# Attention, dense layer and routed experts on one core: moving a logarithm to GpSimd, loading the first head pair on two queues, and gathering the first expert's rows before the last token group is finished

## The chip, the cores and the metric

The kernel runs on one core of one Trainium2 chip. Its time is the device time in microseconds (us) of one execution, and the number quoted is the median over several executions. The engines of the core are TensorE (PE; its weight loads are listed as PEld), VectorE (DVE), ScalarE (ACT), GpSimd (POOL) and SyncE (SP, which here only starts DMA transfers).

## The reference

Three layers follow each other, all in float32. `B, H, S, D` are 4, 8, 576, 64; there are 2304 tokens of 512 numbers, a dense layer of width 2048, and 8 experts of width 1024 that take exactly 288 tokens each.

```python
scores = q @ k.T / sqrt(D);  cum = cumsum(log(clip(f, 1e-4, 1)))
scores = where(causal, -1e9, scores + cum[:, None] - cum[None, :])
attn   = exp(scores - max);  attn /= attn.sum(-1) + 1e-9
x = (attn @ v) as (2304, 512)
h = x @ w_in;  x = max(0.01 * h, h) @ w_out
# routing: all (token, expert) logits x @ w_gate in falling order; a token goes to
# the first expert in that order that still has room, 288 tokens per expert
out[mask_e] = relu(x[mask_e] @ w1[e]) @ w2[e]
```

`w_in`, `w_out` and `w_gate` belong to the dense layer and the routing, `w1` and `w2` to the experts. `w_in` and `w_out` arrive as float64 and are turned into float32 on the chip by integer operations.

## The kernel before

Most products are made of three float32r products of high and low parts (high by high, high by low, low by high), so that each float32 operand is first split: a copy to float32r is the high part, a subtraction the low part.

**Attention.** It works on 16 pairs of heads. For each pair `prepare` loads k and q, transposes them on PE, splits them into `kh, kl, qh, ql`, and loads two rows of the cumulated logarithm into `kr`. `offsets` makes the scores with queries on the partitions, takes the maxima on DVE (`kept`, `nm`) and the sums of the exponentials on ACT (`sm`), and then the logarithm of the sums: `guess` (DVE), `ratio` (ACT, an exponential) and `series` (DVE, six small operations on a tile `ln` of 128x10). `rows` transposes the result and writes it by DMA into `qr`. `attend` makes the scores again with keys on the partitions, now with the offset already in the product, exponentiates them on ACT (`P`), clears what is not causal on GpSimd, multiplies with v, and `finish` splits the result (`xt`) and stores it. Meanwhile the first half of `w_in` is decoded from float64, partly on DVE (`wbits`), partly on GpSimd (`wsq`, `wst`, low part of `wh`).

All of this is written as operations of a `Plan` with an engine, a duration, needs and a rank. `Plan.order` simulates the engines and rings of buffers and so fixes the order of instructions on each engine; on the chip each engine keeps that order. The constants `ZP` to `ZB` are the ranks, `MW`, `ZW`, `DW` the places of the decoding.

At the start, the zeros and ones that pad `qr`, `kr`, `kh`, `kl`, `qh`, `ql` are set by GpSimd (`pads`). The logarithm of f is cumulated, negated, split and written to DRAM (`cumd`), from where `kr` of each pair is loaded.

**Dense layer.** A first half of the width is computed after the attention and stored to DRAM (`gd`), then a second half is computed and kept in SBUF (`g1s`). Both are multiplied with `w_out` later, by the generator `deferred`: 9 groups of 256 tokens, 96 matmuls of 128x512 each, 864 in all. Groups 0 to 6 are taken one by one, groups 7 and 8 together. Every finished group is copied to `xo` by ACT and stored to `x2d` in DRAM.

**Routing.** The generator `routing` finds the assignment with many small DVE operations and small matmuls. It yields estimated nanoseconds. After each yield, as many matmuls of `deferred` are put into PE's stream as fit: `PACE` times the estimate, divided by 228 ns (lines 1035 to 1042). What is left comes after the routing. The result is `ids`, 96x24 token numbers, three columns per expert.

**Experts.** `fetch(e)` loads and splits the weights of an expert, `gather(e)` fetches its 288 rows of `x2d` by three indirect DMAs from GpSimd's queue, `turn` transposes them on PE into the operand `X[e]`, and `first` (tile `h`) and `after` (tile `y`) are the two products. For expert 0 all of that begins after the last store of `x2d`; the rows of each further expert are gathered while the expert before it is computed.

## Time and profile before

| | |
|---|---|
| median of 3 runs | 941.02 us (940.88 to 943.09) |
| the profiled execution, its own time | 943.13 us |
| its span (first to last instruction) | 941.10 us |
| PE, PEld, DVE, ACT, POOL busy | 95%, 81%, 65%, 43%, 47% of the span |
| mean granted TensorE clock | 0.979 of full speed |

The span is made of stages that follow each other: attention to 213 us, the dense layer's first products to 454 us, routing with the deferred products to 696 us, and the experts to the end. Busy shares are means over these stages, which have different limits; they have to be read stage by stage. A matmul's end is modelled, so that a busy PE is not necessarily a PE at its peak.

### The profile page before, as it was taken

What the parts mean: (1) busy time and instruction counts of PE and PEld (TensorE: products, weight loads), DVE (VectorE), ACT (ScalarE), POOL (GpSimd) and SP (SyncE); (2) the same over time, 40 slices, a digit from 0 to 9 for tenths busy, and PEclk for the clock granted to TensorE, in tenths of its full rate; (3) what the DMA queues carried; (4) which work ended last, traced back from release to release, by engine and by line L of the source; (5) the groups of instructions that cost most, each with busy time, mean ns of one, the idle gap of its engine ahead of it and who ended that gap; (6) DMA issues with size and microseconds to landing.
All of it is one profiled execution on the core that took longest, in us unless ns stands there. A gap on an engine that the chain in (4) does not pass through costs nothing.

```text
span 941.1 us, 19011 instructions
## 1 busy us (share of the span) xinstructions
PE 893.4 (95%) x6906; PEld 759.8 (81%) x6906; DVE 609.9 (65%) x1552; ACT 407.2 (43%) x949; POOL 438.4 (47%) x548
## 2 busy tenths in 40 slices
PE   6899899999999999999999999999959999999996
PEld 5688787887877887777777777777649999999996
DVE  6899999845789369523466766667735666566631
ACT  5988778861222223312222222123314555555521
POOL 8265666345999149100645655468752122221101
PEclk9999999999999999999899999999889999999998
DMA  5455565369985473521212221121336556556511
GB/s 130 105 156 157 143 161 141 95 196 294 334 298 173 156 222 117 178 90 45 85 62 69 68 68 49 65 68 49 116 126 192 175 187 193 191 185 204 182 41 33
DMA packets 139677, 131.81 MB, mean 140 GB/s; under 512 B 68448, under 2 KB 106656, under 8 KB 139584
## 3 DMA queue, kind: packets, MB, share of 16 engines
q1 hardware_dynamic: 136512, 121.17, 41.8%
q0 software_dynamic: 3072, 9.44, 3.4%
q8 instruction: 54, 0.88, 0.4%
q14 instruction: 39, 0.32, 0.1%
HBM read 99.85 MB, written 30.56 MB: 139 GB/s over the span
## 4 chain that ended last, share of the span: by engine, by line
PE 69%; DVE 11%; issue 11%; POOL 4%; ACT 3%; DMA 1%; POOLq 0%; SPq 0%; ACTq 0%; DVEq 0%
PE acc L1031 21%; PE h L71 21%; PE h L1087 7%; PE s L71 7%; PE y L1100 6%; PE T L71 3%; DVE kept L71 3%; DVE ln L71 3%; PE q_ct L1031 2%; DVE wbits L71 2%; ACT kept L71 2%; POOL out L1108 1%; DVE r_ge L1249 1%; DVE xt L71 1%; PE T L1077 1%
## 5 line engine op out<-in xcount | busy, mean ns | idle before, releaser
L71 PE MATMUL h<-X,wh 128*128 128x512 f32 (+1 forms) x960 | 211.1, 376 | 0.9 <-DVE g L71 0.9
L71 PEld LDWEIGHTS h<-X,wh 128*128 128x128 f32 x960 | 166.1, 189 | 38.4 <-DVE g L71 3.0
L1031 PE MATMUL acc<-wh,gh 128*128 128x512 f32 x576 | 190.3, 406 | 0.0
L461 POOL TENSOR_TENSOR gl<-g,gh 128x512 fp32r<-128x512 f32 x64 | 104.1, 1631 | 75.5 <-ACT gh L460 72.3
L1031 PEld LDWEIGHTS acc<-wh,gh 128*128 128x128 f32 x576 | 108.8, 193 | 19.5
L1087 PE MATMUL h<-XE,wh 128*128 128x288 f32 x768 | 118.3, 303 | 0.3 <-ACT XE L1078 0.3
L71 DVE TENSOR_TENSOR wh<-wst,wh 128x512 fp32r<-128x512 f32 x132 | 90.5, 707 | 42.8 <-ACT wh L360 31.2
L1031 PE MATMUL acc<-wh,gl 128*128 128x512 f32 x288 | 116.9, 406 | 0.0
L360 ACT CAST wh<-wst 128x512 fp32r<-128x512 f32 x132 | 80.4, 621 | 79.9 <-DMA wst<-in_moe_w 47.2
L1087 PEld LDWEIGHTS h<-XE,wh 128*128 128x128 f32 x768 | 106.5, 191 | 0.6 <-ACT XE L1078 0.6
L460 ACT CAST gh<-g 128x512 fp32r<-128x512 f32 x64 | 39.5, 621 | 141.6 <-PE acc L1031 127.1
L71 ACT ACTIVATE g<-h 128x512 f32<-128x512 f32 (+1 forms) x72 | 39.5, 551 | 139.0 <-PE h L71 136.8
L1100 PE MATMUL y<-eh,wh 128*128 128x288 f32 x512 | 98.4, 296 | 0.0
L71 ACT ACTIVATE kept<-kept,nm 128x192 f32<-128x192 f32 (+4 forms) x160 | 87.8, 551 | 17.1 <-DVE nm L71 16.9
L1108 POOL DMA_INDIRECT out<-yo,ids x24 | 24.7, 1028 | 129.3 <-DVE yo L1107 120.1
L1100 PEld LDWEIGHTS y<-eh,wh 128*128 128x128 f32 x512 | 79.5, 188 | 0.2 <-ACT eh L1091 0.2
L71 DVE TENSOR_TENSOR g<-g,h 128x512 f32<-128x512 f32 (+1 forms) x72 | 44.6, 621 | 51.9 <-ACT g L71 51.9
L71 DVE SCALAR_TENSOR_TENSOR wbits<-w,wbits 128x256 int32<-128x256 int32 x128 | 75.3, 589 | 2.8
L71 POOL TENSOR_TENSOR wst<-wsq,wbits 128x256 f32<-128x256 f32 x64 | 49.8, 779 | 46.4 <-DVE wbits L71 42.3
L1100 PE MATMUL y<-el,wh 128*128 128x288 f32 x256 | 67.9, 296 | 0.0
L1031 PEld LDWEIGHTS acc<-wh,gl 128*128 128x128 f32 x288 | 55.4, 192 | 9.8
L71 POOL TENSOR_SCALAR wsq<-wsq 128x256 f32<-128x256 f32 x64 | 59.9, 935 | 5.6
(210 smaller groups left out, 1605.3 us busy)
## 6 DMA issues: line engine op xcount, KB each, us to landing
wst<-in_moe_w SPq DMA_DIRECT2D x128, 256.0 KB
X<-xd SPq DMA_DIRECT2D x12, 1024.0 KB
g<-gd SPq DMA_DIRECT2D x36, 256.0 KB
w<-in_moe_w_in SPq DMA_DIRECT2D x32, 256.0 KB
w<-in_moe_w_out SPq DMA_DIRECT2D x32, 256.0 KB
gd<-g SPq DMA_DIRECT2D x16, 512.0 KB
xd<-xt SPq DMA_DIRECT2D x16, 320.0 KB
x2d<-xo SPq DMA_DIRECT2D x18, 256.0 KB
```

Source lines behind the costliest of these rows:

```text
L71: r = getattr(self.engine, name)(*a, **k)
L360: A.copy(r[u][0], x)
L460: A.copy(gh, g)
L461: G.tensor_tensor(gl, g, gh, op=OP.subtract)
L1031: tc.keep_in_program_order(PE.matmul(*a, **k))
L1077: PE.transpose(p[:, M * t:M * t + M], xe[t][:, 128 * c:128 * c + 128], ident[:M, :M])
L1087: PE.matmul(h[:, :CAP], w, X[:, c, x, :], start=n == 0, stop=n == 3 * NC - 1)
L1100: PE.matmul(yt[c][:, :CAP], w[:, s], a, start=j == 0 and n == 0, stop=j == NJ - 1 and n == 2)
L1108: sd = G.indirect_dma_start(out=out[:, :], out_offset=bass.IndirectOffsetOnAxis(ap=ids[:, 3 * e + t:3 * e + t + 1], axis=0), in_=y, in_off ...
L1249: V.scalar_tensor_tensor(many[:, :NT * (K + 1)].rearrange("p (i k) -> p i k", k=K + 1)[:, :, :K], key[:, :, None].to_broadcast(s), base if ...
```

## The change

Seven things change.

1. In `offsets`, the first guess of the logarithm goes from DVE to ACT, and the series from DVE to GpSimd, where it is nine small instructions (one for `ready`, eight for `series`) in place of six.
2. `FIN`: the high part of the first 320 queries of each pair (`xt`) is copied by ACT instead of DVE.
3. For pair 0, q is loaded on ACT's DMA queue while k is loaded on SP's; `kr` of pair 0 is copied straight from the negated tile in SBUF, not from `cumd`; its `KR` pads are set by DVE. The memsets and the load of `w_gate`, and `sel`, move behind the attention.
4. The planner's ranks change, and `PACE` goes from 1.1 to 1.05.
5. `deferred` takes all nine groups one by one. In the last, the low parts of g are made by DVE instead of GpSimd, and its sums stay in PSUM.
6. The rows of the last group in `x2d` are set to zero beforehand. Expert 0's rows are gathered right after `ids`, while the last group is still being multiplied; when all but 24 of its matmuls are in PE's stream, PE transposes them as products with the identity into four PSUM tiles `px`. When the last group is done, its two 128x512 tiles are split (`Y`) and multiplied with one-hot matrices (`sel8`, made from the ranks `df`) into the same `px`: 16 matmuls of 128x288. `px` is then split into the operand `X0`. The stores of the last group to `x2d` come after that.
7. `g1s` becomes one tile per piece of `WIDE2`, so that `ax`, `X0` and `Y` can take the place of finished pieces.

```diff
-ZP, ZO, ZA, ZH, ZL, ZW, DW = -38, -27, 5, -6, -14.5, 68.5, 15.5
-ZS = 7, 3.5, 7, 1, 3.5, 11.5, 15.5
+ZP, ZO, ZA, ZH, ZL, ZW, DW = -39, -27, 5, -9.5, -10.5, 63, 14.5
+ZS = 5, 5.5, 7, 0.5, 2.5, 11, 11.5
-FIN = ("vec", "vec"), ("vec", "gp")
+FIN = ("act", "vec"), ("vec", "gp")
-PACE = 1.1
+PACE = 1.05
+QS = "sp", "aq"
...
-    G.memset(wgs, 0.0)
-    with nc.allow_non_contiguous_dma(reason="small"):
-        nc.sync.dma_start(wgs[:, :, :E], w_gate.rearrange("(c p) e -> p c e", p=128))
...
+            on = (vec, "vec") if n == 0 else (gp, "gp")
...
+            at_q = (sp, act) if n == 0 else (sp, sp)
...
-                sp.dma_start(x3[j][:, :, i], src[b, h + i, :512].rearrange("(t p) d -> p t d", p=128))
+                at_q[j].dma_start(x3[j][:, :, i], src[b, h + i, :512].rearrange("(t p) d -> p t d", p=128))
...
+                if n == 0:
+                    outs[0].append(op("sp", 450, lambda l=u: sp.dma_start(kr[l:l + 65:64, :S].bitcast(FT), pre["cn"][l][:2].bitcast(FT)), [negs[u]] + pads[0], z + 1, (), [sets[0]], 30))
+                    continue
...
-            def guess():
-                own["ln"] = x = at.tile([128, 3, 10], FT, name="ln", tag="ln", bufs=2)
-                vec.tensor_scalar(x[:, 0], own["sm"].bitcast(I32), LN[0], LN[1], op0=OP.mult, op1=OP.add)
-
             def ratio():
-                act.activation(own["ln"][:, 1], own["ln"][:, 0], AF.Exp)
+                own["ln"] = x = at.tile([128, 4, 10], FT, name="ln", tag="ln", bufs=2)
+                act.activation(x[:, 0], own["sm"].bitcast(I32), AF.Copy, scale=LN[0], bias=LN[1])
+                act.activation(x[:, 1], x[:, 0], AF.Exp)
+
+            def ready():
+                x = own["ln"]
+                gp.tensor_scalar(x[:, 3], own["sm"], 1e-9, None, op0=OP.add)
 
             def series():
                 x, t = own["ln"][:, 2], own["ln"][:, 1]
-                vec.scalar_tensor_tensor(t, own["sm"], 1e-9, t, op0=OP.add, op1=OP.mult)
-                vec.tensor_scalar(x, t, LN[5], LN[4], op0=OP.mult, op1=OP.add)
-                vec.tensor_tensor(x, x, t, op=OP.mult)
-                vec.scalar_tensor_tensor(x, x, LN[3], t, op0=OP.add, op1=OP.mult)
-                vec.scalar_tensor_tensor(x, x, LN[2], own["ln"][:, 0], op0=OP.add, op1=OP.add)
-                vec.tensor_tensor(x, x, own["nm"][:, :10], op=OP.add)
+                gp.tensor_tensor(t, own["ln"][:, 3], t, op=OP.mult)
+                gp.tensor_scalar(x, t, LN[5], LN[4], op0=OP.mult, op1=OP.add)
+                gp.tensor_tensor(x, x, t, op=OP.mult)
+                gp.tensor_scalar(x, x, LN[3], None, op0=OP.add)
+                gp.tensor_tensor(x, x, t, op=OP.mult)
+                gp.tensor_scalar(x, x, LN[2], None, op0=OP.add)
+                gp.tensor_tensor(x, x, own["ln"][:, 0], op=OP.add)
+                gp.tensor_tensor(x, x, own["nm"][:, :10], op=OP.add)
...
-        for gs in [[g] for g in range(NG - 2)] + [[NG - 2, NG - 1]]:
+        for g in range(NG):
...
+                    gh, gl = split_g(x, V if g == NG - 1 else G)
...
-        for _ in rest:
-            pass
+                dealt.append(1)
+        def deal(n):
+            while len(dealt) < n and next(rest, None):
+                dealt.append(1)
+        deal(96 * NG - 92)
+        ax = g1p.tile([128, 4, 512], FT, name="xe", tag="g1a", bufs=1)
...
+        for t in range(2):
+            V.tensor_scalar(sel8[t], ax[:, 3, :CAP], where[0][:, NT - 2 + t:NT - 1 + t], None, op0=OP.is_equal)
+        gather(0, [ax[:M, t] for t in range(3)])
...
+        deal(96 * NG - 24)
+        for t in range(3):
+            for c in range(NC):
+                mm(px[c][:, M * t:M * t + M], ax[:M, t, 128 * c:128 * c + 128], ident[:M, :M], start=t == 0, stop=False)
+        deal(96 * NG)
+        Y = g1p.tile([128, 4, 2, 512], FR, name="Y", tag="g1b", bufs=1)
+        for t in range(2):
+            A.copy(Y[:, t, 0], last[t])
+            V.tensor_tensor(Y[:, t, 1], last[t], Y[:, t, 0], op=OP.subtract)
+        for l in range(2):
+            for t in range(2):
+                for c in range(NC):
+                    mm(px[c][:, :CAP], Y[:, t, l, 128 * c:128 * c + 128], sel8[t], start=False, stop=l == t == 1)
+        for c in range(NC):
+            part_operand(X0, c, px[c])
+        for t in range(2):
+            leave_first(NG - 1, t, last[t])
...
-        xe = {0: gather(0)}
-        X = {0: operand()}
-        for c in range(NC):
-            turn(X[0], xe[0], c)
+        xe = {}
+        X = {0: X0}
```

## Rows read from the trace of the kernel before

**Rows 1.** Windows by stage: us, busy us (instructions) per engine, granted clock, DMA.

```profile
25.00:205.00 180.00, 165.05 (x1971) 144.39 (x1967) 156.66 (x613) 150.74 (x445) 96.35 (x158) 0.98 0.54 145
454.00:692.60 238.60, 233.98 (x1617) 181.18 (x1614) 160.52 (x353) 57.93 (x97) 147.08 (x124) 0.97 0.22 72
```

**Rows 2.** The chain that ended last, 25 to 205 us, shares by line.

```profile
by line: PE s L71 27.0%; DVE kept L71 16.2%; DVE ln L71 13.6%; issue 9.6%; ACT kept L71 7.4%; DVE wbits L71 6.8%; DVE xt L71 4.4%; DVE ql L71 2.6%; ACT kh L71 1.9%; ACT qh L71 1.8%; DVE nm L71 1.6%; DVE X L71 1.4%; DMA x<-in_k 1.0%; DVE kl 
```

**Rows 3.** Windows inside the attention, columns as in rows 1.

```profile
175.00:200.00 25.00, 24.51 (x314) 21.65 (x312) 19.06 (x79) 21.30 (x60) 9.09 (x20) 1.00 0.62 180
60.00:170.00 110.00, 100.92 (x1213) 88.54 (x1215) 101.29 (x384) 91.13 (x271) 70.02 (x108) 0.98 0.57 152
```

**Rows 4.** Tile ln: ns min/median/max, first and last start.

```profile
L71 DVE SCALAR_TENSOR_TENSOR ln<-ln x32: 169/314/1295, 25.2 to 195.9; 128x10 f32<-128x10 f32 x32
L71 DVE TENSOR_SCALAR ln<-sm x16: 159/166/599, 23.9 to 194.4; 128x10 f32<-128x10 int32 x16
```

**Rows 5.** Tile ln in one window: us, then busy PE, PEld, DVE, ACT, clock, DMA.

```profile
0.00:205.00 205.00, 4.50 (x16) 1.36 (x16) 35.54 (x112) 3.34 (x16) 0.98 0.55 144
```

**Rows 6.** Tiles r_nr and xt, columns as in rows 4.

```profile
L1298 POOL TENSOR_SCALAR r_nr<-r_rp x7: 255/261/403, 489.1 to 673.9; 128x8 f32<-128x8 f32 x7
...
L71 DVE CAST xt<-s x14: 474/479/491, 46.2 to 199.5; 128x320 fp32r<-128x320 f32 x14
```

**Rows 7.** Timeline at 112 us, GpSimd and DVE: start, us, instruction.

```profile
111.99 1.29 POOL L71 TENSOR_TENSOR wh<-wst,wh 128x512 fp32r<-128x512 f32 x1
112.01 1.29 DVE L71 SCALAR_TENSOR_TENSOR ln<-ln 128x10 f32<-128x10 f32 x1
```

**Rows 8.** Timeline of the first 13 us.

```profile
6.42 0.75 DVE L71 SCALAR_TENSOR_TENSOR kept<-cum,kept 32x576 fp32r<-32x576 f32 x1
...
7.15 0.89 SPq L71 DMA_DIRECT2D cumd<-kept  x2
...
8.38 1.55 DVE L71 SCALAR_TENSOR_TENSOR X<-s,X 128x512 fp32r<-128x512 f32 x4 [1.21 <-ACT X L71]
...
11.17 0.59 SPq L71 DMA_DIRECT2D X<-cumd  x2
...
13.01 0.93 PE L71 MATMUL s<-X,qo 64*128 64x192 f32 x2 [0.18 <-POOL qr L71]
```

**Rows 9.** Waits between 460 and 692 us: total us, times, longest.

```profile
DVE r_jk L1258 <- PE q_ct L1031: 49.2, 34, 5.2
...
PEld L1031 <- DVE r_ge L1249: 7.9, 17, 2.5
```

**Rows 10.** Timeline from the routing's last matmuls to expert 0.

```profile
692.20 0.41 PE L1031 MATMUL q_misc<-r_ge 128*96 128x48 bf16 x6
...
692.86 0.18 DVE L71 SCALAR_TENSOR_TENSOR ids<-q_misc,r_kf 96x24 int32<-96x24 f32 x1
...
695.53 0.39 PE L1031 MATMUL acc<-wh,gl 128*128 128x512 f32 x1
699.58 1.17 POOL L1069 DMA_INDIRECT xe<-x2d,ids  x1 [8.23 <-DMA x2d<-xo]
...
703.06 0.56 PE L1077 MATMUL T<-ident,xe 96*128 96x96 f32 x2 [7.14 <-DMA xe<-x2d,ids]
...
705.47 0.58 PE L1077 MATMUL T<-ident,xe 96*128 96x96 f32 x2 [0.70 <-DMA xe<-x2d,ids]
...
709.72 0.40 ACT L1078 CAST XE<-T 128x288 fp32r<-128x288 f32 x1 [1.57 <-PE T L1077]
...
712.46 1.32 PE L1100 MATMUL y<-eh,wh 128*128 128x288 f32 x8
```

**Rows 11.** One window there, columns as in rows 1.

```profile
700.00:708.00 8.00, 3.34 (x13) 2.50 (x14) 0.82 (x2) 0.96 (x3) 5.37 (x6) 0.50 0.46 132
```

**Rows 12.** Pieces of the chain on PE: start us, us, what.

```profile
488.66 11.01 PE acc L1031 x48
...
719.43 1.59 PE y L1100 x12
```

More of the change, by code (lines that the diff above doesn't have):

```diff
@@ L96 @@
            ("vec", "act"): 205, ("vec", "gp"): 155, ("act", "gp"): 180}
-    MOVE = 650, 2200
+    MOVE = 650, 2600
     TURN = 200
@@ L908, in tile_kernel @@
         run(plan)
+        G.memset(wgs, 0.0)
+        with nc.allow_non_contiguous_dma(reason="small"):
+            nc.sync.dma_start(wgs[:, :, :E], w_gate.rearrange("(c p) e -> p c e", p=128))
+        V.tensor_tensor(sel, ident[:, 0:E], ident[:, 32:32 + E], op=OP.add)
+        V.tensor_tensor(sel, sel, ident[:, 64:64 + E], op=OP.add)
+        V.tensor_tensor(sel, sel, ident[:, 96:96 + E], op=OP.add)
+        G.memset(wg2, 0.0)
         stp_.__exit__(None, None, None)
@@ L954, in tile_kernel, with deferred @@
         run(plan)
[L957 to L960 removed]
+    def deferred(mm, last):
+        for g in range(NG):
+            acc = [psa.tile([128, 512], FT, name="acc", tag="acc", bufs=ACB) for _ in range(GT // 128)]
+            if g == NG - 1:
+                last.extend(acc)
             for half in range(2):
                 for i in range(NF // 2):
[L963 to L977 removed]
@@ new lines, in deferred @@
+                    if half:
+                        x = gtp.tile([128, 2, GT], FT, name="g0", tag="g0", bufs=3)
+                        nc.sync.dma_start(x, gd[g][:, 2 * i:2 * i + 2])
+                    else:
+                        x = g1((g,), slice(2 * i, 2 * i + 2))[:, 0]
+                    gh, gl = split_g(x, V if g == NG - 1 else G)
+                    for j in range(2):
+                        w = (wo0 if half else wo)[i]["w"][j]
+                        yield from second(mm, acc, gh[:, j], gl[:, j], w, half == i == j == 0, half == j == 1 and i == NF // 2 - 1)
@@ new lines, in deferred, with leave_first, gather @@
+            if g < NG - 1:
+                for t in range(GT // 128):
+                    leave_first(g, t, acc[t])
+    def leave_first(g, t, acc):
+        xo = gtp.tile([128, DM], FT, name="xo", tag="xo", bufs=2)
+        A.copy(xo, acc)
+        nc.sync.dma_start(x2d[GT * g + 128 * t:GT * g + 128 * t + 128], xo)
+    def gather(e, xe):
+        for t, x in enumerate(xe):
+            G.indirect_dma_start(out=x, out_offset=None, in_=x2d[:, :],
+                                 in_offset=bass.IndirectOffsetOnAxis(ap=ids[:, 3 * e + t:3 * e + t + 1], axis=0))
+        return xe
@@ L979, in tile_kernel, with part_operand @@
+    def part_operand(X, c, p):
+        A.copy(X[:, c, 0], p[:, :CAP])
+        V.tensor_tensor(X[:, c, 1], p[:, :CAP], X[:, c, 0], op=OP.subtract)
+    M = 96
+    keep = ctx.enter_context(tc.tile_pool(name="keep", bufs=1, reuse_waits="tile"))
     with ExitStack() as c2:
         g1p = c2.enter_context(tc.tile_pool(name="g1", bufs=1, reuse_waits="tile"))
-        g1s = [g1p.tile([128, NG - 2, NF, GT], FT, name="g1")]
+        g1s = {}
         def g1x():
@@ L1034, in tile_kernel @@
         wo0 += [{"w": split_weights([(0, 1024, wod[jj])], V)} for jj in range(NF // 4, NF // 2)]
-        rest = deferred(ps, mm)
+        zero = gtp.tile([128, DM], FT, name="xo", tag="xo", bufs=2)
+        G.memset(zero, 0.0)
+        for t in range(GT // 128):
+            nc.sync.dma_start(x2d[NTOK - GT + 128 * t:NTOK - GT + 128 * t + 128], zero)
+        last, where, dealt = [], [], []
+        rest = deferred(mm, last)
         slack = 0
-        for ns in routing(nc, rt, ids, ps, W0, mm, vec):
+        for ns in routing(nc, rt, ids, ps, W0, mm, vec, where):
             slack += PACE * ns
@@ L1063, in fetch @@
             return wa, wb
-        def gather(e):
-            xe = []
-            for t in range(3):
-                x = ep.tile([M, DM], FT, name="xe", tag="xe", bufs=6)
-                G.indirect_dma_start(out=x, out_offset=None, in_=x2d[:, :],
-                                     in_offset=bass.IndirectOffsetOnAxis(ap=ids[:, 3 * e + t:3 * e + t + 1], axis=0))
-                xe.append(x)
-            return xe
         def turn(X, xe, c):
@@ L1126, in tile_kernel @@
                 W[e + 1] = fetch(e + 1)
-                xe[e + 1] = gather(e + 1)
+                xe[e + 1] = gather(e + 1, [ep.tile([M, DM], FT, name="xe", tag="xe", bufs=6) for _ in range(3)])
                 X[e + 1] = operand()
@@ L1144, in tile_kernel, with routing @@
             leave(E - 1, ys, t)
-def routing(nc, wk, ids, ps, W0, mm, vec):
+def routing(nc, wk, ids, ps, W0, mm, vec, where):
     V, G = nc.vector, nc.gpsimd
@@ L1318, in routing @@
     best(df, inc, OP.add)
+    where.append(df)
     na = T("na", NT)
```

106 lines of the change are left out of this document (47 added, 59 removed).

## The prediction, made before the change was built or run

> **What bounds the kernel now.** I read the windows by stage first, then, inside each stage that the change touches, the chain, the waits and the timeline. In the attention PE is busy for 165.1 of 180 us and DVE for 156.7 [rows 1], and the chain there goes back and forth between them: 27% on PE, but 13.6% on the small DVE operations on `ln` and 16.2% on the maxima `kept` [rows 2]. The reader is to see two engines that are both nearly full and wait for each other. The first guesses start at 23.9 and the last at 194.4 [rows 4], so a pair takes 170.5/15 = 11.37 us. Between 60 and 170 us this period holds 10.43 us of PE, 10.47 of DVE, 9.42 of ACT and 7.24 of GpSimd (each busy time times 11.37/110) [rows 3].
>
> In the routing stage PE is busy for 234.0 of 238.6 us [rows 1]. DVE waited 49.2 us there for the counts `q_ct`, while PE's weight loads waited 7.9 us for DVE [rows 9]: the deferred matmuls in front of the counts set the pace, not the search on DVE.
>
> Between routing and experts nobody is full. The last deferred matmul ends at 695.92; then come the stores, the gather from 699.58, the transposes from 703.06, and `y` of expert 0 begins at 712.46 [rows 10]. PE stood idle for 7.14 us, and from 700 to 708 us its granted clock was 0.50 [rows 11], the 1.2 GHz level. From the end of the deferred matmuls to the first `y` are 16.5 us.
>
> **Start (pair 0).** The first product with `kr` runs at 13.01 although the last low part of pair 0 ended at 9.93: `kr` was written to DRAM at 7.15 and read back from 11.17 on [rows 8]. The copy from SBUF needs only the negated rows, the second of which ends at 7.17, and the pads, of which three fewer stand in GpSimd's queue. The read took 13.01 - 11.17 = 1.84 us from issue; 7.3 + 1.84 gives 9.1. Then the low parts are last, at 9.93. Loads of k and q on two queues may bring them forward by up to 1 us, but three memsets come to DVE in front of them, so I leave 9.93. The gain is 13.0 - 9.9 = 3.1 us, of which something may be lost again when pair 1 is late next: its `kr` still goes over `cumd`. Bounds 0 and 4, taken 3. The load of `w_gate` and its memsets, moved past the attention, cost nothing: `wgs` is used more than 20 us later, under the first products of the dense layer; without that cover it would be one transfer, some 2 us.
>
> **Attention, removed and added.** The tile `ln` costs DVE 35.54 us in 112 instructions [rows 5], 2.22 us a pair; the copy of `xt` 0.48 more [rows 6]. DVE falls to 10.47 - 2.70 = 7.77 us a pair. ACT gets one more activation of 128x10 (3.34/16 = 0.21 [rows 5]) and a copy of 128x320, for which I take the 0.40 of the nearest cast, 128x288 [rows 10]: 10.03. GpSimd gets nine instructions of 128x10; the nearest, 128x8 in the routing, has 0.26 [rows 6]: 2.3, together 9.6. PE stays at 10.43. So PE becomes the longest, and the period can fall from 11.37 at most to 10.43, over 15 periods 14.1 us; the other bound is 0. In the one window in which DVE was not full (19.1 of 25 us, at 175) PE was busy for 24.5 of 25 [rows 3], which speaks for a large part; but PE, ACT and GpSimd would then stand at 10.4, 10.0 and 9.6 in engines that keep a fixed order, and what is late next is whichever waits behind another's instruction: on ACT the exponentials `P` behind the new copy, on GpSimd the causal masks, for which PE's product with v waits, behind the nine. I take a third, 0.31 us a pair, that is 5 us. The logarithm itself may come later without harm, since the planner places the second scores of a pair 32 ranks (nearly three pairs) behind the first.
>
> What speaks against it are the rows at 112 us: a GpSimd subtraction and a DVE operation on `ln` begin 0.02 us apart and both last 1.29 us [rows 7], where that DVE operation takes 0.169 alone [rows 4]. The two engines hold each other up. The DVE copy of `xt` from PSUM, min to max 0.474 to 0.491 [rows 6], was never held. Most DVE work of the attention reads PSUM, and the `ln` operations, which were held the most, are those that leave. So I charge DVE nothing. The Trainium skill says the same more sharply ("SBUF — State Buffer", SBUF: two separate sides): the two share a port pair as an exclusive lock for a whole instruction; and it warns ("Perfetto Trace Analysis", Optimizing Scalar/DVE Operations) that moving work between them might not help. By that rule at its worst each added instruction would cost DVE its own length, 16 x 2.3 = 37 us, all that DVE gains, and the attention's term would be about 0.
>
> **Routing and the step to the experts.** The yields in `routing` sum to 176,179 ns (5,000, seven phases of 23,197, and 8,800 at the end); times 1.1 over 228 are 850 of the 864 matmuls, times 1.05 are 811. So 53 instead of 14 remain for the end. One costs 11.01/48 = 0.229 us [rows 12]. Since PE sets the pace, the routing ends 39 x 0.229 = 8.9 us earlier; bounds 0 (if the search on DVE became the limit) and 8.9. In its small steps PE already waits now and then (17 times [rows 9]), so I take 8.4. From the routing's last matmuls (692.6) to the first `y` are now 19.9 us [rows 10]. After the change that stretch holds:
>
> - 53 matmuls, 12.1 us. The gather starts at once behind `ids`, 0.4 us after those matmuls end, and from its first issue to the transposes of its last rows went 699.58 to 705.47, 5.9 us [rows 10]; the 29 matmuls in front of the transposes last 6.6. So at most 0.8 us of waiting.
> - 12 transposes as plain products, a form that the trace does not show at this size: between 0.13 each, a product of 288 columns (1.59/12 [rows 12]), and 0.29, a transpose at half clock (0.58/2 [rows 10]); 1.6 to 3.5, and 1.9 because the clock is full here.
> - From the last matmul: by length from 320 columns on DVE in 0.48 and 288 on ACT in 0.40 [rows 6, 10], a tile of 512 takes 0.77 and 0.71. The first tile is copied under the last three matmuls; the two subtractions follow each other, 1.5, then the last four of the 16 products, 0.5, and three hand-overs between engines of some 0.2: 2.7. First tile of `X0`: copy 0.40, subtraction 0.43; then 24 products `h`, 3.2, under which the other tiles are made. Together 6.7 us.
>
> Sum 12.1 + 0.8 + 1.9 + 6.7 = 21.5, 1.6 more than now, against 8.4 won before: 6.8 us. With the idle of 7.14 us gone, the clock has no cause to fall to 0.50, so I price everything here at full rate. What may be late next is expert 0's weights: their buffers come free with the last group alone, not with two, so 12 subtractions on GpSimd fall into the last 20 us beside the gather; and expert 1's gather, which now waits for the last stores after `X0`. I take 0.3 us off: 6.5, bounds -2 and 10.
>
> The low parts made by DVE in the last group (8 of about 0.8 us) lie under 96 matmuls of 22 us; the zeros written to `x2d` under 200 us of matmuls; without that cover they would cost some 3 us. Taking groups 7 and 8 apart costs PE nothing, the count stays 864.
>
> **Sum.** 3 + 5 + 6.5 = 14.5 us. Against the profiled execution, 941.1 of span and 943.1 in all, that is 926.6 and 928.6; the median of the runs shown lies 2.1 below its time, so I predict **926.5**.
>
> **Rivals.** (a) *GpSimd fills the attention's gain*: the nine instructions stand in front of the causal masks and the decoding, and the period stays 11.37. For it: GpSimd at 9.6 of 11.37 with 1.3 us subtractions in its order; against it: 4 us idle per pair now. Only start and step are left: 941.0 - 9.5 = 931.5. (b) *The step gains nothing*: the search on DVE limits the routing once PE has fewer matmuls to put in (bound 0 above), so the longer tail is paid in full: 941.0 - 8 + 1.6 = 934.6. For it: 17 waits of PE for `r_ge`; against: 49 us of DVE waiting for PE. (c) *Slower: GpSimd becomes the bound.* If its nine instructions are held by DVE as `ln` was held by GpSimd, each takes longer; at (11.37 - 7.24)/9 = 0.46 us the attention gains nothing, and from 0.60 us the kernel is slower by more than 0.3%: 7.24 + 5.4 = 12.6 a pair over the ten pairs of the decoding is 13 us lost, 941.0 - 9.5 + 13 = 944.5. The Trainium skill's lock ("SBUF — State Buffer", SBUF: two separate sides) would work in this direction as well, since whoever begins first keeps the pair; how often, only the trace of the changed kernel can show. (d) *The attention runs at PE's pace*: the whole 14.1, and 917.4.
>
> **Chances.** The forecast 0.55 (its own range 920 to 933), (a) 0.15, (b) 0.13, (c) 0.07, (d) 0.10. The range 916 to 938 holds all but (c) and the edges of (b) and (d). 0.3% is 2.8 us, about what a measurement of this kernel can tell from no change: under 938.2 lie the forecast, (a), (d) and most of (b), 0.88; within it 0.06; above 943.8 most of (c), 0.06.
>
> **What would show it.** The first product with `kr` near 10 us; first to last logarithm about 166 us apart instead of 170.5, with DVE near 70% busy and GpSimd over 80%; the GpSimd instructions on `ln` near 0.26 us; the routing's last matmul some 12 to 17 us earlier on the clock (start, attention and pace together); from the last deferred matmul to the first `y` about 7 us instead of 16.5, with no window at 0.50. GpSimd operations on `ln` of half a microsecond, PE waiting for `P` from GpSimd, transposes waiting for the gather, or a routing stage no shorter than before would make the prediction wrong.

## The result, and the profile after

The changed kernel takes 925.42 us (924.36 to 927.42, four runs) against 942.06 us (940.88 to 943.10, four runs) of the kernel before beside it: 0.9825 of the time [95% 0.9809 to 0.984], 16.6 us less. The median lies 1.1 us under the forecast of 926.5 us and inside its range. The profiled execution took 927.42 us, with a span of 925.7 us, 15.4 less than before; what follows is read from it.

Where the 15.4 us came from is seen best at points that both traces have. Each line gives the time of the point, and how far the new kernel is ahead there:

| point | before | after | ahead |
|---|---|---|---|
| first product with `kr` | 13.01 | 11.11 | 1.9 |
| first logarithm | 23.9 | 19.8 | 4.1 |
| last logarithm | 194.4 | 182.7 | 11.7 |
| first routing product with `sel` | 454.0 | 442.7 | 11.3 |
| last product from `r_ge` of the routing | 692.4 | 672.7 | 19.7 |
| first `y` of expert 0 | 712.46 | 694.59 | 17.9 |
| last of the eight rounds of `y` of expert 0 | 735.49 | 720.11 | 15.4 |

So the start gave 4.1, the attention 7.6, the routing 8.4; the step to the experts took back 1.8, and expert 0 another 2.5. The dense layer in between lost 0.4.

These are differences between two single executions, and some of them are looser than they look. The kernel of run 2 below has the attention of the kernel before, and its first product `h` of the dense layer came at 215.4 instead of 213.4; so a part of the start or the attention is good to some 2 us. Two parts are firmer. From the first product with `sel` to the last from `r_ge` the routing took 235.9 to 239.7 us in the four traces with the old `PACE`, and 228.0 to 231.7 in the ten with the new one. From the first `y` of expert 0 to the end, the three traces with the old step took 228.3 to 228.7 us, and the ten with the new one 230.9 to 233.4 (run 12, with another order there, 229.5).

**The attention.** The windows of the changed kernel (us, busy us with instructions for PE, PEld, DVE, ACT and GpSimd, granted clock, DMA share, GB/s), beside [rows 1] and [rows 3]:

```profile
25.00:205.00 180.00, 172.27 (x2057) 148.88 (x2058) 118.43 (x480) 159.08 (x469) 129.56 (x303) 0.98 0.57 154
60.00:170.00 110.00, 107.31 (x1324) 94.17 (x1322) 81.69 (x332) 105.12 (x318) 86.93 (x199) 1.00 0.56 149
```

From 60 to 170 us PE is now busy for 107.31 of 110 us, 98% where it was 92%, and DVE for 81.69 where it was 101.29. The logarithms are (182.7 - 19.8)/15 = 10.86 us apart, 11.37 before. The chain from 25 to 205 us, by line, shows the same:

```profile
by line: PE s L72 45.7%; issue 7.6%; POOL ln L72 7.1%; POOL wsq L72 7.0%; POOL P L72 6.2%; DVE kept L72 5.6%; ACT kept L72 3.9%; POOL wst L72 3.6%; POOL xt L72 3.6%; DMA w<-in_moe_w_out 3.0%; POOL wh L72 2.1%; PE h L72 1.5%; ACT P L72 1.5%;
```

In [rows 2] PE's `s` had 27.0% and DVE's `ln` and `kept` nearly 30% together; now `s` has 45.7%, and what DVE keeps is 5.6%. In its place GpSimd appears with `ln`, `wsq`, `P`, `wst`, `xt` and `wh`, some 30%. The waits between 25 and 200 us say what is left in front of PE (total us, times, longest):

```profile
DVE kept L72 <- PE s L72: 22.5, 16, 2.6
...
PEld s L72 <- POOL P L72: 4.3, 14, 1.5
...
PEld s L72 <- DVE xr L72: 2.4, 2, 2.2
...
PE s L72 <- POOL P L72: 1.7, 3, 1.3
...
PE s L72 <- DVE nm L72: 1.5, 3, 1.1
...
PEld s L72 <- POOL ln L72: 1.2, 4, 0.5
```

DVE now waits for PE: 22.5 us for the scores, where it was 2.1. The single tile that PE's weight loads wait for longest is now GpSimd's `P`, though DVE's `xr` and `nm` are still there as well. Before, PE and its weight loads waited for `nm` of DVE (25 to 205 us):

```profile
PE s L71 <- DVE nm L71: 10.5, 19, 2.0
```
```profile
PEld s L71 <- DVE nm L71: 13.9, 18, 2.2
```

**The instructions on `ln`**, tile view (ns min/median/max, first and last start), beside [rows 4]:

```profile
L72 POOL TENSOR_TENSOR ln<-ln x64: 202/206/211, 20.4 to 185.5; 128x10 f32<-128x10 f32 x64
L72 POOL TENSOR_SCALAR ln<-ln x48: 204/240/249, 20.7 to 185.2; 128x10 f32<-128x10 f32 x48
L72 POOL TENSOR_SCALAR ln<-sm x16: 239/254/446, 19.6 to 183.4; 128x10 f32<-128x10 f32 x16
L72 ACT ACTIVATE ln<-sm x16: 193/200/214, 19.8 to 182.7; 128x10 f32<-128x10 int32 x16
```

On GpSimd nearly every one has its shortest time, where DVE's went from 169 to 1295 ns. How they stand in GpSimd's order is seen on its timeline (start, us, instruction):

```profile
93.56 0.20 POOL L72 TENSOR_TENSOR ln<-ln 128x10 f32<-128x10 f32 x1
93.85 0.20 POOL L72 TENSOR_SCALAR ln<-ln 128x10 f32<-128x10 f32 x1
94.14 0.21 POOL L72 TENSOR_TENSOR ln<-ln 128x10 f32<-128x10 f32 x1
...
95.65 0.21 POOL L72 TENSOR_TENSOR ln<-ln,nm 128x10 f32<-128x10 f32 x1
95.81 1.48 POOL L72 TENSOR_SCALAR_AFFINE_SELECT P<-P 128x256 f32<-128x256 f32 x4
```

Each lasts 0.20 to 0.24 us, but they start 0.30 us apart, (95.65 - 93.56)/7, since each needs the one before it. The causal masks of `P`, which PE needs next, follow right behind.

**The start.** The read of `kr` for pair 0 starts at 8.68, from SBUF, instead of at 11.17, from DRAM, and the first product with `kr` comes when the last low part (`X<-s,X` on DVE) and the products in front of it are through:

```profile
8.68 0.63 SPq L72 DMA_DIRECT2D X<-kept  x1
...
8.93 1.55 DVE L72 SCALAR_TENSOR_TENSOR X<-s,X 128x512 fp32r<-128x512 f32 x4 [0.66 <-ACT X L72]
...
10.37 0.61 PE L72 MATMUL s<-X 64*128 64x192 f32 x6 [0.46 <-DVE X L72]
11.11 0.36 PE L72 MATMUL s<-X,qo 64*128 64x192 f32 x2
```

The second queue did not bring the transposes forward: PE's first ones of pair 0 start at 5.84, where they started at 5.17. Of what was to move behind the attention, only the load of `w_gate` did (issued at 21.4 instead of 1.25); the memset of `wgs` and the three operations on `sel` stand there in the program, but in the trace they still run at 0.93 and between 1.96 and 4.9.

**The step to the experts.** The timeline of the changed kernel, beside [rows 10]:

```profile
673.20 0.18 DVE L72 SCALAR_TENSOR_TENSOR ids<-q_misc,r_kf 96x24 int32<-96x24 f32 x1
...
673.68 1.19 POOL L997 DMA_INDIRECT xe<-x2d,ids  x1 [0.37 <-DVE ids L72]
...
679.47 0.58 PE L1059 MATMUL q_ct<-ident,xe 96*128 96x96 f32 x4
...
687.42 0.39 PE L1059 MATMUL acc<-wh,gl 128*128 128x512 f32 x1
687.80 0.53 PE L1059 MATMUL q_ct<-XE,Y 128*128 128x288 f32 x2
...
691.29 3.46 PE L1141 MATMUL h<-XE,wh 128*128 128x288 f32 x24 [0.95 <-DVE XE L1003]
694.59 1.22 PE L1154 MATMUL y<-eh,wh 128*128 128x288 f32 x8
697.57 0.36 PE L1132 MATMUL T<-ident,xe 96*128 96x96 f32 x2 [1.76 <-DMA xe<-x2d,ids]
```

The gather starts 0.3 us behind `ids`, and the transposes at 679.47 wait for nothing. From the last matmul of the last group to the first `y` are 694.59 - (687.42 + 0.39) = 6.8 us, where there were 16.5. The window from 673 to there has the full clock, where [rows 11] had 0.50:

```profile
673.00:694.60 21.60, 20.65 (x118) 17.83 (x118) 12.14 (x15) 11.11 (x21) 12.55 (x12) 1.00 0.46 153
```

Right in front of this window the routing's end got worse: PE waited 2.87 us for a product on GpSimd up to 669.15 (1.87 before), and from 669 to 673 us the granted clock was 0.57 on the mean, where the kernel before kept 1.00 through its routing's end (690 to 698 us).

The last line of the timeline is the other part that went worse. After the first eight `y` of expert 0, PE's order holds the transposes of expert 1's rows, whose gather could start only at 692.65, behind the late stores of the last group. PE waited 1.76 us there with all of expert 0's products behind it.

### The profile page after: what moved, and what is told of

The parts are those of the page before. It is cut to its first block, busy times and chain, and to the rows that moved or that the text cites. A ratio compares the mean times of both kernels' runs of the same rounds, so it can differ in the third digit from the quotient of the medians.

```text
span 925.7 us, 19093 instructions
## 1 busy us (share of the span) xinstructions
PE 889.4 (96%) x6934; PEld 755.8 (82%) x6934; DVE 584.0 (63%) x1439; ACT 416.6 (45%) x983; POOL 457.6 (49%) x683
## 4 chain that ended last, share of the span: by engine, by line
PE 69%; issue 11%; POOL 10%; DVE 4%; ACT 2%; DMA 2%; SPq 0%; POOLq 0%; DVEq 0%; ACTq 0%
PE acc L1059 21%; PE h L72 19%; PE s L72 9%; PE h L1141 6%; PE y L1154 6%; POOL wsq L72 3%; PE T L72 3%; PE q_ct L1059 2%; POOL wst L72 2%; POOL ln L72 1%; ACT kept L72 1%; DVE r_ge L1301 1%; DVE kept L72 1%; POOL P L72 1%; POOL out L1162 1%
## 5 line engine op out<-in xcount | busy, mean ns | idle before, releaser
L1059 PE MATMUL acc<-wh,gh 128*128 128x512 f32 x576 | 188.2, 404 | 0.0
L452 ACT CAST gh<-g 128x512 fp32r<-128x512 f32 x72 | 44.5, 621 | 155.0 <-PE acc L1059 132.5
L72 ACT ACTIVATE g<-h 128x512 f32<-128x512 f32 (+1 forms) x80 | 44.4, 555 | 154.4 <-PE h L72 154.4
L72 DVE TENSOR_TENSOR g<-g,h 128x512 f32<-128x512 f32 (+1 forms) x80 | 50.2, 629 | 68.6 <-ACT g L72 68.2
L72 DVE CUSTOM_DVE_ANT_0 kept<-s,mask 128x192 f32<-128x192 f32 (+4 forms) x160 | 59.2, 426 | 23.0 <-PE s L72 22.5
L72 POOL TENSOR_TENSOR wst<-wsq,wbits 128x256 f32<-128x256 f32 x64 | 49.6, 775 | 36.4 <-DVE wbits L72 31.5
```

Source lines behind the costliest of these rows:

```text
L72: r = getattr(self.engine, name)(*a, **k)
L452: A.copy(gh, g)
L1059: tc.keep_in_program_order(PE.matmul(*a, **k))
```

## The experiments

Ratios are against runs of the kernel before on the same chip; its median there was 942.15 to 942.76 us. The changed kernel was timed beside it at 942.06, so that the medians can be set against its 925.42. The intervals reach some 1.5 to 2.7 us to either side, so that a difference of 3 us between two runs is at their edge.

**1. The attention alone.** The kernel before with parts 1 to 4 of the change, but the old tail and the old `PACE`; parts 5 to 7 are left out.

```diff
-ZR = 5
+ZR = 5.5
...
 PACE = 1.1
```

> The changes of the attention alone (log series on GpSimd, FIN, pair 0, ranks), with the old routing pace, the old deferred groups and expert 0's gather after the last store. In the trace of the changed kernel the dense layer's first product comes 11.7 us earlier. Theory (the parts add up and nothing gives the attention's gain back): 941.5 - 11.7 = 930, within 928 to 931.5. Rival (the dense layer's decoding of w_out or the routing absorbs part of the earlier start): 933 or more. My own terms of the prediction, 3 + 5, would give 933.5.

Measured 928.93 us, 0.9865 [0.9839 to 0.989]: 13.6 us gained. That is inside what the theory expected. The dense layer's first `h` starts at 201.9, as in the changed kernel (201.7).

**2. The step alone.** The kernel before with parts 5 to 7 and `PACE` 1.05.

```diff
-PACE = 1.1
+PACE = 1.05
...
-        xe = {0: gather(0)}
+        xe = {}
+        X = {0: X0}
```

> The other half alone: PACE 1.05, nine single groups, the last group's low parts on DVE, expert 0's rows gathered early and completed by one-hot products; the attention as before. Theory: the routing ends 8 to 8.9 us earlier, the stretch to expert 0's first y is some 2 us longer and expert 0 itself some 2 us longer, because its PE stream waits for expert 1's gather: 941.5 - 4 = 937.5, within 936 to 939. My prediction's term was 6.5, which would be 935. Rival (b), the step gains nothing: 941 or more.

Measured 938.34 us, 0.9973 [0.9957 to 0.999]: 4.2 us gained. 13.6 and 4.2 make 17.8, the whole change 16.6: the two halves add up within what the intervals allow.

**3. The logarithm alone.** The kernel before with part 1 only, with its old ranks.

```diff
-            o = op("vec", 80, guess, tots, z + ZR, ["ln"], [sb])
+            o = op("act", 450, ratio, tots, z + ZR, ["ln"], [sb])
...
-            o = op("vec", 900, series, [p], z + ZR, (), [nb, sb, lb])
+            o = op("gp", 2200, series, [o, p], z + ZR, (), [nb, sb, lb])
```

> The kernel before with only the guess on ACT and the series on GpSimd; old ranks, old FIN. Theory: 3 to 7 us faster than before, 934.5 to 938.5, as the period falls from 11.37 towards 11. Rival (port contention takes back what DVE gains, as in the skill's rule at its worst): no change, 940 or more. A third possibility: the old ranks fit the old durations and hold the order back, 939 to 941.

Measured 932.73 us, 0.9907 [0.9882 to 0.9932]: 9.8 us gained by the medians, 7.6 between the spans of the profiled executions (941.1 and 933.5), more than was expected. Its logarithms run from 23.8 to 186.7, 10.86 us apart as in the changed kernel. So this one part is enough for the whole gain in the period, as far as single executions tell: the four traces with the changed attention have 10.73 to 10.99. The other parts show elsewhere: this run's first `h` comes at 207.9, 6.2 us behind the changed kernel's, of which 4.0 are there at the first logarithm and 2.2 come behind the last.

**4. The logarithm back on DVE**, in the changed kernel (part 1 undone).

```diff
-            o = op("gp", 2200, series, [o, p], z + ZR, (), [nb, sb, lb])
+            o = op("vec", 900, series, [p], z + ZR, (), [nb, sb, lb])
```

> The changed kernel with the guess and the series of the logarithm back on DVE, all else as changed (ranks, FIN, pair 0, step). Theory (the 35 us of DVE are what limited the attention): DVE goes back to near 10 us a pair beside PE, and the time rises by 5 to 8 us, to 930.5 to 933.5. Rival (new ranks, FIN and pair 0 made the gain, the place of the series does not matter): within 2 us of 925.4.

Measured 947.89 us, 1.0064 [1.0043 to 1.0084]: 22 us slower than the changed kernel, and slower than before. The direction was expected, the size was not: the logarithms run from 20.1 to 201.3, 12.08 us apart, longer than the 11.37 of the kernel before. The explanation that fits is that the new ranks are made for the new places and are worse than the old ones with the old places; the copy of `xt` on ACT may have a part in it, and the two were not tried apart.

**5. The old ranks** in the changed kernel (`PACE` stays at 1.05).

```diff
-ZP, ZO, ZA, ZH, ZL, ZW, DW = -39, -27, 5, -9.5, -10.5, 63, 14.5
+ZP, ZO, ZA, ZH, ZL, ZW, DW = -38, -27, 5, -6, -14.5, 68.5, 15.5
...
-NEAR = 10
+NEAR = 11
```

> The changed kernel with the old ranks (ZP to ZB, ZT, ZR, MW, NEAR). The log alone with old ranks gave 9.8 us, the whole attention 13.6. Theory: the ranks are worth little by themselves, 926 to 929. Rival (the order must fit the new places of the work): 931 or more.

Measured 935.55 us, 0.9929 [0.9906 to 0.9953], 10 us slower than the changed kernel, as the rival had it. From 60 to 170 us its PE was busy for 102.21 us instead of 107.31, and the period is (187.3 - 19.4)/15 = 11.19. Run 3 has the old ranks as well and keeps 10.86; so the old ranks do not seem to suit the rest of the new attention (the copy of `xt` on ACT, pair 0). This is argued from two runs, and which rank it is was not tried. At the first `h` (207.9) the run is 6.2 us behind; the rest comes later, in stages whose code is the same, and is not explained.

**6. The copy of `xt` back on DVE**, in the changed kernel.

```diff
-FIN = ("act", "vec"), ("vec", "gp")
+FIN = ("vec", "vec"), ("vec", "gp")
```

> The changed kernel with the high part of the first 320 queries copied by DVE again (FIN as before), all else as changed. Theory (DVE is no longer full, ACT nearly is): DVE gets 0.48 us a pair back and ACT loses 0.40; within 2 us of 925.4. Rival (what moved off DVE matters by its length, as the series does): 0.48 x 16 = 8 us slower, 930 to 934.

Measured 928.35 us, 0.9863 [0.9837 to 0.9889], 2.9 us above the changed kernel, between what the theory and the rival expected. The intervals overlap, so more is not shown; in its trace the period is 11.10 and the first `h` 2.8 us later, which points the same way.

**7. Pair 0 as before**, in the changed kernel: one queue, `kr` by way of `cumd`, pads on GpSimd.

```diff
-            at_q = (sp, act) if n == 0 else (sp, sp)
+            at_q = (sp, sp)
...
-            on = (vec, "vec") if n == 0 else (gp, "gp")
+            on = (gp, "gp")
```

> The changed kernel with pair 0 as before: k and q on SP's queue, kr through cumd, its KR pads on GpSimd. Theory: the first product with kr comes some 3 us later and all that follows with it, 927.5 to 929.5 (my term was 3; the trace shows 1.9 at that product and 4.1 at the first logarithm). Rival (a late first pair is absorbed in the attention, where PE then finds more work ready): within 1 us of 925.4.

Measured 928.81 us, 0.9858 [0.9838 to 0.9878]: 3.4 us above the changed kernel, where the forecast's term for the start was 3. The first logarithm is at 22.2 instead of 19.8. But the two intervals touch, the first `h` of the dense layer is only 0.7 us later (202.4), and the first `y` of expert 0 is not later at all (694.2 against 694.59). So the rival, that the attention absorbs a late first pair, is not refuted: the medians speak against it, the one trace for it. The first logarithm itself varies: runs 10 and 11, with the new start, have it at 21.1 and 21.2.

**8. The series doubled on GpSimd.** Behind each of the nine instructions of the changed kernel stands a second that writes a part of `ln` that is no longer needed; the result is the same.

```diff
                 gp.tensor_tensor(t, own["ln"][:, 3], t, op=OP.mult)
+                gp.tensor_tensor(own["ln"][:, 3], t, t, op=OP.mult)
                 gp.tensor_scalar(x, t, LN[5], LN[4], op0=OP.mult, op1=OP.add)
+                gp.tensor_tensor(own["ln"][:, 3], t, t, op=OP.mult)
```

> The changed kernel with each of the nine GpSimd instructions of the logarithm followed by one more of the same size into a scratch column: 144 more, some 32 us of GpSimd, order unchanged. Between 60 and 170 us GpSimd is busy for 86.9 of 110 us now; this makes it about 107. Theory (GpSimd has room, the latency of the logarithm is hidden): 0 to 5 us slower, 925 to 930. Rival (c) of the prediction (GpSimd is at its edge): 10 us slower or more, 935 and up.

Measured 939.57 us, 0.9973 [0.9954 to 0.9992], 14 us above the changed kernel, where 925 to 930 were expected. Its logarithms run from 19.9 to 194.5, (194.5 - 19.9)/15 = 11.64 us apart. Window, GpSimd's timeline and waits of this run:

```profile
60.00:170.00 110.00, 100.23 (x1200) 86.03 (x1197) 75.53 (x306) 96.78 (x288) 95.52 (x266) 0.97 0.53 140
```
```profile
97.03 0.57 POOL L72 TENSOR_SCALAR ln<-sm 128x10 f32<-128x10 f32 x2
...
98.39 0.49 POOL L72 TENSOR_TENSOR ln<-ln 128x10 f32<-128x10 f32 x2
...
101.44 1.49 POOL L72 TENSOR_SCALAR_AFFINE_SELECT P<-P 128x256 f32<-128x256 f32 x4
```
```profile
PEld s L72 <- POOL ln L72: 9.5, 11, 2.0
PEld s L72 <- POOL P L72: 7.3, 17, 1.9
PE s L72 <- POOL ln L72: 7.0, 7, 1.8
...
PE s L72 <- POOL P L72: 3.5, 6, 1.7
```

The eighteen take up 0.57 + (101.44 - 98.39) = 3.6 us a pair, where the nine take 0.33 (92.53 to 92.86) and 2.25 (93.56 to 95.81), 2.6. PE falls from 107.31 to 100.23 busy us, and waits for GpSimd in four places. But PE and its weight loads wait longer for `ln` itself (16.5 us) than for the masks behind it (10.8), so this run alone does not tell a late logarithm from a full GpSimd.

**9. Nine more, but behind the series.** The same load, placed so that the logarithm is not late; only what follows it in GpSimd's order is.

```diff
                 gp.tensor_tensor(x, x, own["nm"][:, :10], op=OP.add)
+                for _ in range(9):
+                    gp.tensor_tensor(own["ln"][:, 3], t, t, op=OP.mult)
```

> The changed kernel with nine more GpSimd instructions of 128x10 per pair, put behind the last one of the series into a scratch column: the same occupancy of GpSimd as doubling each (144 more, 32 us), but the logarithm itself comes no later. Doubling each cost 14 us. Theory 1 (the logarithm comes later than the place in PE's order that the planner gave its transposition, so the latency is what costs): most of the 14 us vanish, 926 to 931. Theory 2 (GpSimd's order is full, so that its masks and decoding come late): the cost stays, 935 to 941.

Measured 956.91 us, 1.016 [1.0137 to 1.0183], 31.5 us above the changed kernel and more than either theory expected. Its timeline on GpSimd and its waits:

```profile
105.49 0.21 POOL L72 TENSOR_TENSOR ln<-ln,nm 128x10 f32<-128x10 f32 x1
105.65 2.44 POOL L72 TENSOR_TENSOR ln<-ln 128x10 f32<-128x10 f32 x9
108.05 1.49 POOL L72 TENSOR_SCALAR_AFFINE_SELECT P<-P 128x256 f32<-128x256 f32 x4
```
```profile
PEld s L72 <- POOL P L72: 18.8, 25, 2.5
PE s L72 <- POOL P L72: 12.9, 13, 2.3
...
PEld s L72 <- POOL ln L72: 2.7, 10, 0.8
...
PE s L72 <- POOL ln L72: 0.9, 2, 0.6
```

The nine keep the masks back by 2.4 us, and PE waits for `P`, hardly for `ln`. The period is (205.8 - 19.7)/15 = 12.41 us. So the time taken up in GpSimd's order is enough to cost all this, with the logarithm on time; that its lateness cost nothing in run 8 is not shown. The order has room for the nine instructions and for hardly more. It was made, in runs 8, 9 and 10, without knowledge of the added instructions; whether another order would hold them better was not tried. Runs 8 and 9 add the same number of instructions; in run 8 a part of them falls into the gaps of 0.09 us between dependent ones, so that it takes up 1.0 us more a pair, run 9 2.4 us. The periods grew by 0.78 and 1.55 us, some 0.7 per us taken up, and the times by 14 and 31.5 (12.7 and 26.5 between the spans).

**10. The time given back to DVE.** Seven small two-input operations on a spare tile per pair, in the changed kernel, behind the low part of each pair's transposed logarithm.

```diff
                 vec.tensor_tensor(mine[1][:, 1], mine[0], mine[1][:, 0], op=OP.subtract)
+                for _ in range(7):
+                    vec.tensor_tensor(spare[:, :10], spare[:, 10:], spare[:, 10:], op=OP.mult)
```

> The changed kernel with seven two-input DVE operations of 128x10 per pair on a scratch tile, behind the low part of each pair's transposed logarithm: the number and size of operations that the logarithm had on DVE before, but with nothing that waits for their result. Theory (what the change removed from DVE was occupancy): DVE rises from 74% towards 92% and 5 to 14 us come back, 930 to 939. Rival (it was the chain through DVE, ACT and DVE that cost): under 3 us.

Measured 936.62 us, 0.995 [0.9929 to 0.9971], 11.2 us above the changed kernel, inside what was expected. The 112 operations, which nobody waits for, took 27.6 us:

```profile
L72 DVE TENSOR_TENSOR spare<-spare x112: 147/170/1196, 27.8 to 197.4; 128x10 f32<-128x10 f32 x112
```

DVE is busy for 90.70 us from 60 to 170, 82% where some 92% had been expected, and that is enough: the period is (191.9 - 21.1)/15 = 11.39, where the kernel before has 11.37. So time taken up on DVE is by itself enough to lose the gain, without a logarithm that comes late. Small DVE operations still last up to 1.2 us.

**11. The old pace**, in the changed kernel: 14 deferred matmuls instead of 53 are left for the early gather to hide behind.

```diff
-PACE = 1.05
+PACE = 1.1
```

> The changed kernel with PACE 1.1: 850 instead of 811 deferred matmuls go in before the routing ends, 14 are left. Theory (the early gather needs the matmuls behind ids as cover): the routing ends 8.9 us later; the gather's 6 to 7 us lie open in front of the transposes, and PE has only 14 matmuls left after them: 5 to 7 us slower, 930 to 933. Rival (the order of the same PE work does not matter): within 1.5 us of 925.4.

Measured 939.05 us, 0.9971 [0.9953 to 0.9988], 13.6 us above the changed kernel, twice what was expected. PE's timeline, and three windows:

```profile
681.37 0.64 PE L1059 MATMUL q_misc<-r_ge 128*96 128x48 bf16 x6
687.89 1.17 PE L1059 MATMUL q_ct<-ident,xe 96*128 96x96 f32 x4 [5.87 <-DMA xe<-x2d,ids]
```
```profile
678.00:682.00 4.00, 4.00 (x21) 3.04 (x20) 1.36 (x1) 0.52 (x1) 4.00 (x4) 0.50 0.01 3
682.00:688.00 6.00, 0.13 (x2) 0.12 (x1) 0.36 (x2) 0.62 (x1) 4.24 (x4) 0.50 0.78 244
688.00:698.00 10.00, 10.00 (x37) 9.00 (x38) 0.00 (x0) 0.21 (x1) 0.00 (x0) 0.54 0.05 16
```

The wait of 5.87 us was expected. Not expected was the clock: from 688 to 698 us PE was busy for all of 10 us, but at a granted clock of 0.54, near the 1.2 GHz level, where the changed kernel has 1.00; that is 10 x 0.46 = 4.6 us of work lost. The wait of 5.87 us did not bring the clock down. It had fallen before, while PE waited 3.46 us for a product on GpSimd up to 677.63, and stood at 0.50 through the 4 us of work from 678 on, through the wait, and up to 697. In the changed kernel it had fallen at the same place, at 669, and was back at 1.00 from 673 on, with the deferred matmuls following without a gap. So the two together, 5.9 + 4.6 = 10.5, are nearly all of the 10.7 us by which the first `y` (705.25 against 694.59) and the span (936.4 against 925.7) are behind. The medians are 13.6 apart because the profiled execution of the changed kernel took 2.0 more than its median, and this one (938.23) 0.8 less.

**12. A better version?** The changed kernel with expert 0's PE instructions kept in the order of the program (`pe`, which is not sorted anew, so that no transposes of expert 1 stand among expert 0's first products), and one routing product moved from GpSimd to DVE.

```diff
-                PE.transpose(p[:, M * t:M * t + M], xe[t][:, 128 * c:128 * c + 128], ident[:M, :M])
+                T[0].transpose(p[:, M * t:M * t + M], xe[t][:, 128 * c:128 * c + 128], ident[:M, :M])
...
+            T[0] = PE if e else pe
...
-    G.tensor_scalar(oa[:, :, 1], ga, ip[:, 0:1], None, op0=OP.mult)
+    V.tensor_scalar(oa[:, :, 1], ga, ip[:, 0:1], None, op0=OP.mult)
```

> The changed kernel with two edits. PE's instructions of expert 0 keep the program's order, so that the transposes of expert 1's rows come behind its third y, not behind the first eight matmuls, where PE waited 1.76 us for that gather. And one product of the routing's end (oa times ip, 128x432) goes from GpSimd to DVE: PE waited 2.87 us for it, as two weight subtractions of 5.9 us stood in front of it on GpSimd. Theory: 1.8 + 1 to 2 us faster, 921.5 to 924. Rivals: the wait moves on to the next late thing (weights, the next subtraction), 924.5 to 926; DVE, at the end of the routing, gets later by the 0.6 us of the product and more.

Measured 927.34 us, 0.9847 [0.9819 to 0.9876]: no better than the changed kernel. The first edit did what it should: the eight rounds of `y` of expert 0 run from 698.37 to 722.18, 23.8 us apart, where the changed kernel needs 25.5. The second did not; the last product of the routing waits even longer:

```profile
662.91 8.16 POOL L360 TENSOR_TENSOR wh<-wst,wh 128x512 fp32r<-128x512 f32 x5 [0.71 <-ACT wh L359]
...
668.62 1.33 DVE L1388 TENSOR_SCALAR r_ge<-r_ga,r_ip 128x432 bf16<-128x432 bf16 x1
669.87 1.66 DVE L1389 TENSOR_TENSOR r_ge<-r_ga,r_mw 128x432 bf16<-128x432 bf16 x1
...
671.59 0.60 PE L1059 MATMUL q_misc<-r_ge 128*96 128x48 bf16 x6 [3.81 <-DVE r_ge L1389]
```

PE waits 3.81 us for DVE there, where it waited 2.87 for GpSimd in the changed kernel. The time from the first product with `sel` to the last with `r_ge` is 1.1 us longer (231.1 against 230.0), the way from there to the first `y` 1.2 longer, and the routing of this execution began 1.5 later, as the attention took longer. The first edit alone was not tried.

## Why the prediction was right, step by step

**The start** was forecast at 3 us and gave 3.4 by the medians of run 7, 4.1 in the trace up to the first logarithm, of which run 7 takes back 2.4; whether all of it reaches the end is open (run 7). That the `kr` read leaves the path and the low parts are last was right; the first product with `kr` came at 11.1 and not at 9.9, since the last low part now ends at 8.93 + 1.55 = 10.5 and six products stand in front. Pair 1, whose `kr` still goes over `cumd`, has its logarithm 2.8 us earlier (26.39 against 29.20), so that 1.3 of the 4.1 were lost again there; up to 40 us the trace puts only 0.2 us of waiting down to `kr`.

**The attention** was forecast at 5 us and gave 7.6 in the trace (9.8 by the medians of run 3). The mechanism was right: DVE fell (to 81.69 of 110 us, 74%; 70% was forecast), PE became the longest (98%), and GpSimd came to 79%, where over 80% was said. The step that was mis-sized is "I take a third" of the 0.94 us between the periods of 11.37 and 10.43: it was 0.51, over a half. The fear was that the fixed orders of ACT and GpSimd give little; GpSimd had just enough room. Rival (a), GpSimd filling the gain, is refuted by run 3; rival (d), the whole 14.1, did not come either.

**The price of the nine instructions** was 0.26 each, 2.3 us a pair. They are busy for 144 of 0.22 us, 2.0 us a pair, but take up 2.6 (the eight of the series 2.25 to 2.27 us in 14 of the 16 pairs), because dependent ones start 0.30 us apart. Rival (c) put the point where the attention gains nothing at 0.46 us per instruction, 4.1 a pair. Runs 8 and 9 test it: the period of before, 11.37, lies between the 10.86 at 2.6 us a pair and the 11.64 at 3.6, on a straight line at 3.25, that is 0.36 us per instruction (an estimate from these three periods). So (c) had the mechanism and the place right (PE waits for the masks `P` in run 9, which is slower than before), with a threshold that was too kind, and it did not come true because hardly anything held GpSimd's operations on `ln` up: 64 of them lie between 202 and 211 ns.

**What DVE and GpSimd do to each other.** The prediction charged DVE nothing for GpSimd's added work, and gave the rule of the Trainium skill ("SBUF — State Buffer", SBUF: two separate sides), of an exclusive lock for a whole instruction, as the reason why it might be 37 us and the attention's term 0. Run 3's 9.8 us refute that worst case. The holding itself is there, and on both engines. DVE's spare operations in run 10 went up to 1196 ns. GpSimd's small ones stayed at 249 ns and below in the changed kernel save for one form that reached 446, but single ones reached 430 in run 3 and 525 in run 10; and its subtractions for the experts' weights, with a median of 1.29 us, went up to 4.18. At 677 us of the changed kernel a DVE subtraction with a median of 0.69 us lasts 5.55 beside four of GpSimd's and ends 0.6 us behind the last of them:

```profile
677.38 5.55 DVE L453 TENSOR_TENSOR gl<-g,gh 128x512 fp32r<-128x512 f32 x1 [2.03 <-ACT gh L452]
677.39 4.97 POOL L360 TENSOR_TENSOR wh<-wst,wh 128x512 fp32r<-128x512 f32 x4
```

In [rows 7] the prediction read two engines that hold each other up; there only DVE was held, since 1.29 us is what that GpSimd subtraction takes in the attention anyway (median 1.30 over eight). That the operations on `ln`, which were held up to 1295 ns, are those that leave DVE was right.

**The routing** was forecast to get 8.4 us shorter, and did: 454.0 to 692.4 are 238.4 us, 442.7 to 672.7 are 230.0. Its last matmul came 19.7 us earlier on the clock, more than the 12 to 17 that were named as a sign, since start and attention gave more. Rival (b), that the search on DVE limits it, is refuted. It came near in one place only: the last products of the routing waited 2.87 us for a product on GpSimd, behind two subtractions that took 5.90 us together, and ran at the lower clock for it.

**The stretch to the first `y`** was forecast at 21.5 us and measured at 694.59 - 672.95 = 21.6. Of its parts the wait of up to 0.8 for the gather did not occur, the 12 transposes took 2.6 instead of 1.9 us (679.47 to 682.07; the trace has each as two instructions, 24 in all, some 0.11 us apart), and the part behind the last matmul was 6.8 where 6.7 had been forecast. That the clock stays up there, an assumption, is shown by the window at 1.00, and run 11 shows what it is worth.

**The step as a whole** was forecast at 6.5 us and gave 4.2 in run 2, and 8.4 - 1.8 - 2.5 = 4.1 in the changed kernel. The term that was mis-sized is "I take 0.3 us off" for expert 0's weights and expert 1's gather: it was 2.5. The prediction named that this gather now waits for the last stores, but did not follow where its transposes stand in PE's order: after the first eight `y` of expert 0, so that PE itself stood still. Run 12 without them has 23.8 us for those rounds, close to the 23.0 of before.

The total came out near by some luck, because the errors have opposite signs: by the trace the start gave 1.1 us and the attention 2.6 more than forecast, the step 2.4 less. With 0.4 lost in the dense layer, 4.1 + 7.6 - 0.4 + 4.1 = 15.4 stand against 14.5.

## What to carry to other kernels

When small operations move to an engine that keeps a fixed order, count the time they take up from start to start, not their durations, and ask what stands right behind them in that order and who waits for it; here GpSimd's order had no room left at 79% busy. Before moving work, look whether the operations that stretch the most are the ones that leave: their mean, not their shortest time, is what is won. A transfer that is started early needs its cover measured in the other engine's work that stands in front of its user, and if the cover is too short, the price is the wait and, where the clock is down, the slow stretch that goes on behind it.

## What the hardware showed that was not expected

- Dependent instructions of 128x10 on GpSimd start 0.30 us apart though each lasts 0.20 to 0.24; nine that write one column and do not read each other's results took 2.44 us, 0.27 each, and in run 8, where all but one of the added ones read nothing of the one before them, sixteen took 3.05 us, 0.19 each.
- Operations of DVE and GpSimd last several times their usual length beside each other, on either engine: two-input DVE operations of 128x10 147 to 1196 ns (run 10), GpSimd subtractions of 128x512 1267 to 4180 ns (changed kernel). GpSimd's operations of 128x10 were hardly touched in the changed kernel (202 to 211 ns); why was not tried.
- In run 11 the granted clock, once down after a wait of 3.46 us, stayed at 0.50 through 4 us of work and a wait of 5.87 us; the fully busy stretch right behind, from 688 to 698 us, ran at 0.54. Wait and slow stretch cost 10.5 us together.
